# Moving a kernel's loads and stores from SyncE's DMA queue to GpSimd's and ScalarE's: attention, mixture of experts and FFN in one program

## The chip, the cores and the metric

The kernel runs on one core of a Trainium2 chip. The core has five engines with an instruction stream each: TensorE (PE, matmuls), VectorE (DVE), ScalarE (ACT), GpSimd (POOL) and SyncE (SP). An engine works through its stream in order; an instruction that must wait for something holds all that stand behind it on that engine. DMAs are issued as instructions of SP, ACT or POOL. The metric is the time of one execution on the device in microseconds; of several runs the median counts.

## The reference

Three stages, each feeding the next, all in float32:

```
attn = softmax(q k^T / 8 + decay(f), causal) v       # 4 batches, 8 heads, 576 positions, head size 64
x    = attn as 2304 tokens of 512
e    = argmax(x w_gate)                              # one of 8 experts for each token
y    = gate(x) * (relu(x w1[e]) w2[e])               # w1: 512 x 1024, w2: 1024 x 512 for each expert
h    = y w_in                                        # 512 x 2048
g    = (a0 + a1 h + a2 h^2 + a3 h^3) / (1 + |b0||h| + |b1| h^2)
out  = g w_out                                       # 2048 x 512
```

The second FFN's weights `w_in` and `w_out` come in float64.

## The kernel before, in words

**Attention.** The 32 heads are taken in 16 pairs (`g` = 0 to 15). For each pair TensorE computes row maxima (`max_pass`, tiles `mx`), then transposed scores (`scores`, tiles `st`, two buffers), ScalarE takes the exponential into `pt`, POOL masks the diagonal, and TensorE multiplies with `v` (`pv`, tile `po`). `v_gate` multiplies `vt` by the gate's weights (tile `vg`). The loads of the next pairs (`rk`, `rq`, `v`, `vt`) and the small copies of the row maxima into `QA` are issued by SP.

**Conversion of the FFN's weights.** `w_in` and `w_out` are cut into 16 pieces. For each, `w64_load` loads 1024 KB of raw 64-bit words, `w64_square` (ScalarE) and four parts of `w64_step` (VectorE) turn it into float32 in the tile `w64m`, which has one buffer, and `w64_store` stores it to `wi_d` or `wo_d` in DRAM. A table `W64` spreads the steps over the pairs; the last 11 steps are put among the expert tiles by a list of zeros and ones, one entry for each place where `do_side()` runs. Once `in_moe` is set, the store isn't issued by the step, but by `w64_store()` at the head of the next tile.

**Routing and experts.** After three batches `tile_map(0, 3)` works out the first 6 token tiles (128 tokens of one expert each); the remaining ones follow after the fourth batch. `fetch_w(0)` then loads the first expert's weights, eight pieces of 512 KB into the tiles `raw0` to `raw7`. `scatter_to` writes the tokens' numbers into a table in DRAM, `fetch_i` and `fetch_x` (POOL) read a tile's numbers and gather its tokens (`xg`), up to five tiles ahead. `tiles()` runs over the tiles `p`: `split_some` splits `raw` into `w_hi` (ScalarE, L1029) and `w_lo` (VectorE, L1030), under a condition, where the expert changes; `h_mm` and `y_mm` are the two matmuls; `store_y(p - 1)` stores the tile before (`y_d` and the token numbers `id_d`, on SP); `fetch_next(p)` issues, under a condition, the next expert's eight loads into `raw` (SP, L497). In each tile two `do_side()` stand after the first half of the matmuls, and one or two at the end. With these inputs 22 tiles run; the branch behind L1152, for more of them, is not taken.

**FFN.** From tile 10 on, `side` holds the steps of `ffn_head`: loads of the first 512 rows of `y_d` and `id_d` (`yl`, `id`), loads of pieces of `wi_d` and `wo_d` into `rw` (four buffers), `split_w` of each (ScalarE casts to `wih` or `woh`, POOL subtracts to `wil` or `wol`), and the transposes of `yl`. After the tiles the FFN runs in five chunks of rows.

**What sets the order.** Every engine runs its instructions in the order in which the program writes them. Each DMA of SP or ACT gets one of eight semaphores DMAHW0 to DMAHW7, in turn and in common; each DMA of POOL one of DMASW0 to DMASW7. A DMA waits until the one that had its semaphore last has landed.

Of the kernel before, what the change touches and what calls it, by code (L numbers as in the profile page):

```python
# [23 lines left out]
E = 8  # L24
# [47 lines left out]
def fused_kernel(tc, q2, k2, v2, f, w_gate, w1, w2, w_in, w_out, a_in, b_in, out):  # L72
    nc = tc.nc
    with ExitStack() as top, tc.manual_schedule():
# [379 lines left out]
        got_i, got_x = set(), set()  # L454
        need = {}

        def fetch_w(p, pieces=range(NP), first=None):
            if p not in need:
                need[p] = expert(p)
            e, nd = need[p]  # L460
            for i in pieces:
                ins = fetch_piece(p, i, e, nd)
                if first is not None:
                    tc.add_manual_dep(ins.ins, first, SYNC, reason="the first tokens come before")


        def fetch_next(p):
            e = nc.sync.value_load(at(t_nx, p), min_val=0, max_val=E - 1)
            nd = nc.sync.value_load(at(t_ndx, p), min_val=0, max_val=1)
            for i in range(NP):  # L470
                fetch_piece(p, i, e, nd)


        def fetch_border(i):
            e = nc.sync.value_load(t_b[0:1, 0:1], min_val=0, max_val=E - 1)
            nd = nc.sync.value_load(t_b[0:1, i:i + 1], min_val=0, max_val=1)
            for k in range(NP):
                fetch_piece(NA, k, e, nd)

        def expert(p):  # L480
            e = nc.sync.value_load(at(t_e, p), min_val=0, max_val=E - 1)
            nd = None
            if p:
                nd = nc.sync.value_load(at(t_need, p), min_val=0, max_val=1)
            return e, nd

        def fetch_piece(p, i, e, nd):
            if True:
                if i < 4:
                    src = w1[ds(e, 1), i * P:(i + 1) * P, :].rearrange("a p f -> (a p) f")  # L490
                    dst = raw[i]
                else:
                    src = w2[ds(e, 1), (i - 4) * 256:(i - 3) * 256, :].rearrange("a (c p) d -> p (a c) d", p=P)
                    dst = raw[i].rearrange("p (c d) -> p c d", c=2)
                if nd is None:
                    return nc.sync.dma_start(out=dst, in_=src)
                return nc.sync.dma_start(out=dst, in_=src, cond=nd)  # L497

        def ffn_head(ffn, pool_, y_d, id_d, wi_d, wo_d):
            F0 = ffn["pool"]
            ffn["w", 0] = [F0.tile([P, 4, 512], F32R, name=f"{n}0") for n in ("wih", "wil", "woh", "wol")]
            ffn["yT", 0] = [F0.tile([P, 4, 512], F32R, name=n) for n in ("yhi0", "ylo0")]
# [3 lines left out]
            def load_w(q, i):  # L508
# [4 lines left out]
                else:  # L513
                    src = wo_d[q * 512 + k * P:q * 512 + (k + 1) * P, :]
                nc.sync.dma_start(out=r, in_=src)
                rw_t[q, i] = r
# [7 lines left out]
            def load_y(ci, chunk, tbs=None):  # L524
# [3 lines left out]
                for tb in range(n // P) if tbs is None else [tbs]:  # L528
                    r = slice(c0 + tb * P, c0 + (tb + 1) * P)
                    t = F0.tile([P, DM], F32, tag="yl", name=f"yl{ci}_{tb}", bufs=4)  # L530
                    nc.sync.dma_start(out=t, in_=y_d[r, :])
                    ffn["y"].append(t)
                    t = F0.tile([P, 1], I32, tag="id", name=f"id{ci}_{tb}", bufs=8)
                    nc.sync.dma_start(out=t, in_=id_d[r, :])
                    ffn["id", ci].append(t)
# [29 lines left out]
        with ExitStack() as sa:  # L565
# [19 lines left out]
            ch = DW.tile([32, 2, S], F32R, tag="w64", name="ch", bufs=2)  # L585
            rq_t, rk_t, v_t, w64_t, w64_done = {}, {}, {}, {}, []

# [77 lines left out]
            def w64_load(i):  # L665
                w = DW.tile([P, 1024, 2], I32, tag="w64", name=f"w64_{i}", bufs=2)
                nc.sync.dma_start(out=w.rearrange("p a b -> p (a b)"), in_=w64_at(i)[0].bitcast(I32))
                w64_t[i] = [w]

            def w64_store():  # L670
                for i in w64_done:
                    nc.sync.dma_start(out=w64_at(i)[1], in_=w64_t.pop(i)[2])
                w64_done.clear()
# [7 lines left out]
            def w64_step(i, part):  # L681
# [15 lines left out]
                else:  # L697
# [3 lines left out]
                    w64_done.append(i)  # L701
                    if not in_moe:
                        w64_store()

# [211 lines left out]

            in_moe = []
            first_x = [lambda p=p: (got_i.add(p), fetch_i(p)) for p in range(2)]
            first_x += [lambda p=p: (got_x.add(p), fetch_x(p)) for p in range(2)]
            W64 = [[0, 0, 0, 0, 0, 1, 0], [0, 1, 0, 1, 1, 0, 0], [0, 2, 0, 0, 2, 0, 0], [0, 2, 0, 1, 1, 0, 1], [0, 1, 1, 0, 1, 0, 0], [1, 1, 1, 0, 1, 0, 0], [1, 1, 0, 1, 1, 0, 0], [0, 1, 1, 1, 1, 0, 0], [1, 1, 1, 0, 1, 0, 0], [1, 1, 1, 0, 1, 0, 0], [0, 1, 1, 0, 1, 1, 0], [1, 1, 1, 1, 0, 0, 0], [1, 1, 1, 0, 1, 0, 0], [0, 0, 1, 0, 0, 0, 0], [0, 1, 0, 1, 0, 0, 0], [1, 1, 0, 0, 0, 1, 0]]  # L920
            for g in range(NG):
# [40 lines left out]
                if n and n % H == 0:  # L962
# [5 lines left out]
                    else:  # L968
                        steps += [slots[0], lambda c=scatters, f=slots[1]: (f(), pool_side.extend(c))]
                        steps.append(lambda: (list(tile_map(0, B - 1)), fetch_w(0), pool_side.extend(first_x)))  # L970
                    side += steps
# [39 lines left out]
            in_moe.append(True)  # L1011
            side += [lambda c=c: do_w64(c) for c in (1, 0, 1, 1, 1, 1, 1, 1, 1, 1, 1, 0, 1)]

# [3 lines left out]
        with ExitStack() as sm:  # L1017
# [39 lines left out]
            def tiles(p0, p1, always=False):  # L1057
# [3 lines left out]
                for p in range(p0, p1):  # L1061
                    if p == 10:
                        assert not side
                        w64_store()
                        st_r.close()
                        ffn["pool"] = pool(st_f, "F0", side="right")
                        side.extend(ffn_head(ffn, pool, y_d, id_d, wi_d, wo_d))
                    if p > p0:
                        store_y(p - 1)
                    w64_store()  # L1070
                    xhi, xlo = xT_t.pop(p)
# [80 lines left out]
            with tc.If(nc.values_load(at(t_start, NSURE), min_val=0, max_val=NT) < NT):  # L1152
                fetch_w(NSURE)
                fetch_ahead(NSURE, NTILE)
                tiles(NSURE, NTILE, always=True)
        st_w.close()


# [180 lines left out]
```

## Time and profile before

| | us |
|---|---|
| median of 3 runs | 1136.57 |
| the three runs | 1136.57, 1142.54, 1129.04 |
| profiled execution | 1128.95 |
| its span, first to last instruction | 1127.4 |
| PE busy in the span | 971.1 |
| DVE busy | 776.9 |
| ACT busy | 600.1 |
| POOL busy | 368.5 |

The attention takes about the first 317 us, the expert tiles run to about 695 us, and the FFN to the end. The rows of the profile that follow further below name a line of the kernel, an engine, and the tiles written and read (`out<-in`). "SPq" is SP's queue of DMA instructions. Idle time in brackets is that of the engine just before the instruction, with what ended it. The granted clock of TensorE is told as a share of full speed: 1.00 is the upper of its two levels, 0.50 the lower.

### The profile page before, as it was taken

The numbers are of one execution on the slowest core, as the hardware profiler recorded it, in microseconds if no ns is written. First come the engines' busy times: TensorE is split into PE (matmuls) and PEld (weight loads), VectorE is DVE, ScalarE is ACT, GpSimd is POOL, SyncE is SP. The second block draws the span as 40 slices with busy tenths as digits, with TensorE's granted clock in tenths as the row PEclk, the third lists the DMA queues.
The fourth block names the chain that finished last, engine by engine and source line by source line (L and its number), as shares of the span: only waits on it lengthen the run. The fifth ranks groups of instructions, "written<-read, shape, count | busy, mean of one in ns | idle before, by whom it ended". The sixth has DMA issues, their size and how long they took to land. (4 is left out here: it accounts for less than half of the span.)

```text
span 1127.4 us, 15936 instructions
## 1 busy us (share of the span) xinstructions
PE 971.1 (86%) x4965; PEld 819.1 (73%) x4965; DVE 776.9 (69%) x1412; ACT 600.1 (53%) x928; POOL 368.5 (33%) x428
## 2 busy tenths in 40 slices
PE   4989998886579873987698988889999999999996
PEld 3878887876557653765576866667888888899995
DVE  6876989977056852652326444999988887798984
ACT  6644654542134441552325344777866666677773
POOL 7663756655213020100320000575412222232222
PEclk9966988978589986998989998899999999999999
DMA  5746576777456666666836823331010020010000
GB/s 189 262 141 240 188 230 216 256 176 90 167 188 74 173 226 224 61 205 212 243 71 130 221 58 132 101 97 46 23 44 4 7 66 1 10 47 1 29 1 29
DMA packets 57231, 137.47 MB, mean 122 GB/s; under 512 B 13279, under 2 KB 13703, under 8 KB 55090
## 3 DMA queue, kind: packets, MB, share of 16 engines
q1 hardware_dynamic: 52576, 125.85, 38.0%
q0 software_dynamic: 4544, 10.52, 4.5%
q8 instruction: 41, 0.67, 0.3%
q14 instruction: 52, 0.43, 0.2%
q10 hardware_dynamic: 18, 0.00, 0.0%
HBM read 171.04 MB, written 23.86 MB: 173 GB/s over the span
## 5 line engine op out<-in xcount | busy, mean ns | idle before, releaser
L1222 POOL TENSOR_TENSOR glo<-s,ghi 128x512 fp32r<-128x512 f32 (+1 forms) x68 | 82.4, 1211 | 258.0 <-ACT ghi L1220 173.3
L1030 DVE TENSOR_TENSOR wlo<-raw,whi 128x1024 fp32r<-128x1024 f32 x88 | 104.4, 1224 | 36.5 <-ACT whi L1029 34.5
L809 PE MATMUL po<-v,pt 128*128 128x80 f32 (+2 forms) x960 | 122.7, 283 | 7.1 <-DVE lgh L820 6.9
L809 PEld LDWEIGHTS po<-v,pt 128*128 128x128 f32 (+2 forms) x960 | 115.3, 194 | 16.3 <-issue 8.2
L1183 PE MATMUL fh<-yhi,wih 128*128 128x512 f32 (+1 forms) x320 | 121.6, 380 | 5.6 <-DVE s L1200 5.5
L1185 PE MATMUL fh<-yhi,wil 128*128 128x512 f32 (+1 forms) x320 | 119.9, 375 | 0.0
L1184 PE MATMUL fh<-ylo,wih 128*128 128x512 f32 (+1 forms) x320 | 119.8, 374 | 0.0
L1237 PE MATMUL o<-woh,glo 128*128 128x512 f32 x288 | 113.8, 395 | 1.5 <-POOL glo L1222 1.5
L1235 PE MATMUL o<-woh,ghi 128*128 128x512 f32 x288 | 113.2, 393 | 0.1
L1236 PE MATMUL o<-wol,ghi 128*128 128x512 f32 x288 | 112.7, 391 | 0.0
L1029 ACT CAST whi<-raw 128x1024 fp32r<-128x1024 f32 x88 | 87.8, 1046 | 41.2 <-DMA raw<-in_dram 39.8
L782 ACT ACTIVATE pt<-st 128x768 f32<-128x768 f32 (+1 forms) x64 | 53.5, 837 | 102.2 <-PE st L779 99.1
L1195 ACT ACTIVATE s<-fh 128x512 f32<-128x512 f32 (+1 forms) x80 | 44.3, 554 | 91.3 <-PE fh L1185 91.3
L1082 PE MATMUL h<-whi,xhi 128*128 128x512 f32 x176 | 77.1, 438 | 17.6 <-ACT whi L1029 14.8
L712 DVE CUSTOM_DVE_ANT_0 junk<-mx,wide 128x512 f32<-128x512 f32 (+3 forms) x128 | 62.3, 487 | 33.9 <-PE mx L729 22.0
L1197 DVE SCALAR_TENSOR_TENSOR s<-s,bab,s 128x512 f32<-128x512 f32 (+1 forms) x80 | 56.4, 705 | 36.9 <-ACT s L1196 36.2
L1082 PE MATMUL h<-whi,xlo 128*128 128x512 f32 x176 | 72.8, 414 | 4.5 <-DVE xlo L1049 4.5
L786 POOL TENSOR_SCALAR_AFFINE_SELECT pt<-pt 128x128 f32<-128x128 f32 x144 | 45.3, 342 | 94.5 <-ACT pt L782 93.5
L434 POOL DMA_INDIRECT xg<-x_d,idx x22 | 27.9, 1270 | 140.9 <-DVE ys L1135 111.2
L1095 DVE TENSOR_TENSOR hlo<-ht,hhi 128x512 fp32r<-128x512 f32 x44 | 30.3, 688 | 61.9 <-ACTq L1038 46.6
L1086 ACT ACTIVATE hs<-h 128x512 f32<-128x512 f32 x44 | 26.2, 595 | 87.6 <-PE h L1082 87.5
L1183 PEld LDWEIGHTS fh<-yhi,wih 128*128 128x128 f32 x320 | 60.9, 190 | 15.4 <-DVE s L1200 5.9
(227 smaller groups left out, 2427.6 us busy)
## 6 DMA issues: line engine op xcount, KB each, us to landing
raw<-in_dram SPq DMA_DIRECT2D x200, 512.0 KB
w<-in_dram SPq DMA_DIRECT2D x16, 1024.0 KB
rk<-in_dram SPq DMA_DIRECT2D x16, 576.0 KB
rq<-in_dram SPq DMA_DIRECT2D x16, 576.0 KB
v<-in_dram SPq DMA_DIRECT2D x16, 368.5 KB
y_d<-ys SPq DMA_DIRECT2D x22, 256.0 KB
vt<-in_dram SPq DMA_DIRECT2D x16, 320.0 KB
yl<-y_d SPq DMA_DIRECT2D x18, 256.0 KB
```

What stands on the lines that cost most here:

```text
L712: nc.vector.tensor_tensor_reduce(out=junk[:, :n], in0=in_, in1=mask, scale=1.0, scalar=-3e38, op0=ALU.add, op1=ALU.max, accum_out=out_)
L809: nc.tensor.matmul(po[:BS[i], i, :w], lhsT=pt[r, c:c + BS[i]], rhs=v[r, (h * NB + j) * VW:(h * NB + j) * VW + w], start=(j == 0), stop=(j ...
L1029: nc.scalar.copy(out=w_hi[i], in_=raw[i])
L1030: nc.vector.tensor_tensor(out=w_lo[i], in0=raw[i], in1=w_hi[i].bitcast(F32), op=ALU.subtract)
L1082: nc.tensor.matmul(t, lhsT=x[:, k * P:(k + 1) * P], rhs=w[k][:, c], start=(i == 0), stop=(i == 11))
L1183: nc.tensor.matmul(t[:, :n], lhsT=whi[:, k, c], rhs=hi[:, k, :n], start=(k == 0), stop=False)
L1184: nc.tensor.matmul(t[:, :n], lhsT=whi[:, k, c], rhs=lo[:, k, :n], start=False, stop=False)
L1185: nc.tensor.matmul(t[:, :n], lhsT=wlo[:, k, c], rhs=hi[:, k, :n], start=False, stop=(k == 3))
L1222: eng.tensor_tensor(out=lo, in0=s3, in1=hi.bitcast(F32), op=ALU.subtract)
L1235: nc.tensor.matmul(t, lhsT=hi[:, s], rhs=whi[:, c], start=(u == 0), stop=False)
L1236: nc.tensor.matmul(t, lhsT=hi[:, s], rhs=wlo[:, c], start=False, stop=False)
L1237: nc.tensor.matmul(t, lhsT=lo[:, s], rhs=whi[:, c], start=False, stop=(u == NU - 1))
```

## The change

Four things are edited. `fetch_w(0)` is issued by ScalarE in place of SP. Once `in_moe` is set, `w64_load` and `w64_store` are issued by POOL, and the store comes right behind the step that finishes its tile; the list that places the last 11 steps is another. While `ffn["head"]` is set, which it is until the tiles are done, the loads of `yl`, `id` and `rw` are issued by POOL. In the branch that is not taken the experts' loads lose their condition.

```diff
+        def fetch_w(p, eng=nc.sync):
+            e = eng.value_load(at(t_e, p), min_val=0, max_val=E - 1)
+            for i in range(NP):
+                fetch_piece(i, e, None, eng)
...
-                    return nc.sync.dma_start(out=dst, in_=src)
-                return nc.sync.dma_start(out=dst, in_=src, cond=nd)
+                    return eng.dma_start(out=dst, in_=src)
+                return eng.dma_start(out=dst, in_=src, cond=nd)
...
-                nc.sync.dma_start(out=r, in_=src)
+                (nc.gpsimd if ffn["head"] else nc.sync).dma_start(out=r, in_=src)
                 rw_t[q, i] = r
...
-                    nc.sync.dma_start(out=t, in_=y_d[r, :])
+                    eng = nc.gpsimd if ffn["head"] else nc.sync
+                    eng.dma_start(out=t, in_=y_d[r, :])
...
-                    nc.sync.dma_start(out=t, in_=id_d[r, :])
+                    eng.dma_start(out=t, in_=id_d[r, :])
...
             def w64_load(i):
-                nc.sync.dma_start(out=w.rearrange("p a b -> p (a b)"), in_=w64_at(i)[0].bitcast(I32))
+                eng = nc.gpsimd if in_moe else nc.sync
+                eng.dma_start(out=w.rearrange("p a b -> p (a b)"), in_=w64_at(i)[0].bitcast(I32))
...
             def w64_store():
                 for i in w64_done:
-                    nc.sync.dma_start(out=w64_at(i)[1], in_=w64_t.pop(i)[2])
+                    eng = nc.gpsimd if in_moe else nc.sync
+                    eng.dma_start(out=w64_at(i)[1], in_=w64_t.pop(i)[2])
...
                     w64_done.append(i)
-                    if not in_moe:
-                        w64_store()
+                    w64_store()
...
-                        steps.append(lambda: (list(tile_map(0, B - 1)), fetch_w(0), pool_side.extend(first_x)))
+                        steps.append(lambda: (list(tile_map(0, B - 1)), fetch_w(0, nc.scalar), pool_side.extend(first_x)))
...
-            side += [lambda c=c: do_w64(c) for c in (1, 0, 1, 1, 1, 1, 1, 1, 1, 1, 1, 0, 1)]
+            side += [lambda c=c: do_w64(c) for c in (1, 1, 1, 0, 0, 1, 1, 1, 1, 0, 0, 1, 1, 1, 1)]
...
             F0 = ffn["pool"]
+            ffn["head"] = True
...
         st_w.close()
+        ffn["head"] = False
...
                 for p in range(p0, p1):
                     if p == 10:
                         assert not side
-                        w64_store()
...
                     if p > p0:
                         store_y(p - 1)
-                    w64_store()
```

The first place is the end of the attention, where the first expert's weights are loaded. On SP before, between the copies of the row maxima of the last pair but one and of the last one:

```order
L761 DMA QA_157<-mm_2472 1x9x128 [waits DMAHW0_49,DVE_49]
L481 TENSOR_LOAD te_100 [waits DVE_49]
...
L496 DMA raw_85<-in_dram 128x1024 [waits DMAHW1_49]
...
L496 DMA raw_86<-in_dram 128x1024 [waits DMAHW2_49]
...
L496 DMA raw_92<-in_dram 128x2x512 [waits DMAHW0_49]
L622 DMA v_2583<-in_dram 128x737 [waits DMAHW1_49,PE_49]
L623 DMA vt_2584<-in_dram 128x640 [waits DMAHW2_49]
L761 DMA QA_147<-mm_2690 1x9x128 [waits DMAHW3_49,Activation_49]
L761 DMA QA_147<-mm_2690 1x9x128 [waits DMAHW4_49,DVE_49]
```

On SP now (raw_85 to raw_92 are the tiles raw0 to raw7):

```order
L752 DMA QA_157<-mm_2472 1x9x128 [waits DMAHW1_49,DVE_49]
L612 DMA v_2583<-in_dram 128x737 [waits DMAHW3_49,PE_49]
L613 DMA vt_2584<-in_dram 128x640 [waits DMAHW5_49]
L752 DMA QA_147<-mm_2690 1x9x128 [waits DMAHW3_49,Activation_49]
L752 DMA QA_147<-mm_2690 1x9x128 [waits DMAHW4_49,DVE_49]
```

And on ACT now, where before the exponential of `st_0_2620` followed the copy of `v_2340` at once:

```order
L624 COPY v_2340<-vg_2499 128x5x2x8 [waits DMAHW0_49,PE_49]
L457 TENSOR_LOAD te_100 [waits DVE_49]
...
L484 DMA raw_85<-in_dram 128x1024
...
L484 DMA raw_86<-in_dram 128x1024 [waits DMAHW2_49]
...
L484 DMA raw_89<-in_dram 128x2x512 [waits DMAHW7_49]
...
L484 DMA raw_90<-in_dram 128x2x512 [waits DMAHW0_49]
...
L484 DMA raw_91<-in_dram 128x2x512 [waits DMAHW1_49]
...
L484 DMA raw_92<-in_dram 128x2x512 [waits DMAHW2_49]
L773 ACTIVATE pt_164<-st_0_2620 128x768 [waits PE_49,Pool_49]
```

The eight loads left SP, where `v` and `vt` moved ahead of them, and stand on ACT ahead of the exponentials of the pair. raw_90 waits for the semaphore that raw_85 has, raw_92 for that of raw_86.

The second place is the conversion among the expert tiles. On SP before, one of the stores stood behind two sets of eight loads of `raw` and the store of a tile:

```order
L497 DMA raw_92<-in_dram 128x2x512 [waits DMAHW3_49]
...
L1054 DMA y_d<-ys_4114 128x512 [waits DMAHW4_49,DVE_49]
...
L1055 DMA id_d<-idx_3137 128x1 [waits DMAHW5_49,DMASW0_49]
L672 DMA wo_d<-w64m_4039 128x1024 [waits DMAHW6_49]
```

On POOL now, that load and store stand among the gathers of tokens:

```order
L434 DMA xg_3738<-x_d,idx_3723 128x513 [waits DMASW1_49,DVE_49]
...
L658 DMA w_14_3821<-in_dram 128x2048 [waits DMAHW7_49]
...
L664 DMA wo_d<-w64m_3895 128x1024 [waits DVE_49]
...
L425 DMA idx_3908<-table 128x1 [waits DMAHW4_49,DMASW7_49]
L434 DMA xg_3910<-x_d,idx_3736 128x513 [waits DMASW3_49,PE_49]
```

The store moved ahead of both sets of `raw` loads and off their queue. Behind it on POOL, the next read of token numbers waits for VectorE's last step.

The third place is tile 10 and the ones after it, where the FFN's first loads are made. On POOL now:

```order
L434 DMA xg_4800<-x_d,idx_4634 128x513 [waits DMASW2_49,PE_49]
...
L521 DMA yl_0_4894<-y_d 128x512 [waits DMAHW3_49,DMASW6_49,Activation_49]
L524 DMA id_0_4896<-id_d 128x1 [waits DMAHW4_49]
L504 DMA rw_0_4898<-wi_d 128x512 [waits DMASW0_49]
...
L511 TENSOR_TENSOR wil_4809<-rw_0_4898,wih_4808 128x512 [waits Activation_49]
...
L504 DMA rw_4_5156<-wo_d 128x512 [waits DMASW4_49,Pool_49]
L511 TENSOR_TENSOR wil_4809<-rw_1_4904,wih_4808 128x512 [waits Activation_49]
...
L434 DMA xg_5171<-x_d,idx_4993 128x513 [waits DMASW7_49,DMASW6_49,DVE_49]
...
L504 DMA rw_5_5252<-wo_d 128x512 [waits Pool_49]
```

Before, these loads stood on SP, each behind the eight loads of `raw` of its tile; POOL's stream held the subtractions and gathers alone. A load of `rw` now waits on POOL itself for the subtraction that frees its buffer.

## Rows read from the trace of the kernel before

**Rows 1.** Windows of 50 us: busy time and number of instructions of each engine.
```profile
core 0: us, PE busy (x) PEld busy (x) DVE busy (x) ACT busy (x) POOL busy (x), PEclk, DMA share, GB/s
250.00:300.00 50.00, 29.88 (x200) 27.98 (x199) 23.01 (x87) 10.63 (x15) 18.39 (x33) 0.74 0.74 147
400.00:450.00 50.00, 27.66 (x106) 21.25 (x106) 20.87 (x22) 14.29 (x19) 6.07 (x6) 0.73 0.64 225
800.00:850.00 50.00, 50.00 (x223) 40.83 (x222) 43.77 (x64) 35.55 (x60) 13.17 (x15) 1.00 0.12 38
```

**Rows 2.** TensorE's timeline around its longest waits; idle time and releaser in brackets.
```profile
start us, us, engine line op out<-in xcount [idle before <-releaser]
...
269.01 0.80 PE L729 MATMUL mx<-KA,QA 128*128 128x512 f32 x1 [4.15 <-DVE M L712]
...
271.42 0.47 PE L777 MATMUL st<-QB,KB 128*128 128x192 f32 x1
...
293.18 2.37 PE L632 MATMUL vg<-wg,vt 128*128 128x64 f32 x10 [15.47 <-DMA vt<-in_dram]
...
447.12 1.12 PE L1092 MATMUL ht<-ident,hs 128*128 128x128 f32 x4 [17.27 <-ACT hs L1086]
...
500.75 0.83 PE L1092 MATMUL ht<-ident,hs 128*128 128x128 f32 x4 [4.83 <-ACT hs L1086]
...
526.45 1.11 PE L1092 MATMUL ht<-ident,hs 128*128 128x128 f32 x4 [7.93 <-ACT hs L1086]
...
564.03 1.12 PE L1092 MATMUL ht<-ident,hs 128*128 128x128 f32 x4 [8.83 <-ACT hs L1086]
```

**Rows 3.** ScalarE's timeline: one exponential, and three of its waits.
```profile
264.96 0.81 ACT L782 ACTIVATE pt<-st 128x768 f32<-128x768 f32 x1 [5.53 <-PE st L779]
...
445.46 1.12 ACT L678 ACTIVATE w64m<-w 128x1024 f32<-128x1024 f32 x1 [18.23 <-DMA wo_d<-w64m]
...
525.28 0.62 ACT L521 CAST wih<-rw 128x512 fp32r<-128x512 f32 x1 [9.38 <-DMA rw<-wi_d]
...
562.20 1.29 ACT L521 CAST woh<-rw 128x512 fp32r<-128x512 f32 x2 [9.59 <-DMA rw<-wo_d]
```

**Rows 4.** SP's timeline: issues of DMAs between 265 and 551 us.
```profile
265.35 6.62 SPq L496 DMA_DIRECT2D raw<-in_dram  x8
...
275.67 0.97 SPq L622 DMA_DIRECT2D v<-in_dram  x1
...
277.04 0.35 SPq L623 DMA_DIRECT2D vt<-in_dram  x1
...
283.42 1.83 SPq L761 DMA_DIRECT2D QA<-mm  x2
...
416.89 11.91 SPq L497 DMA_DIRECT2D raw<-in_dram  x16
...
431.62 0.33 SPq L672 DMA_DIRECT2D wo_d<-w64m  x1
...
550.90 4.12 SPq L515 DMA_DIRECT2D rw<-wo_d  x3
```

**Rows 5.** SP's waits, 250 to 350 us: in total, times, longest.
```profile
SPq L761 <- DMA raw<-in_dram: 6.2, 2, 6.0
SPq L622 <- DMA raw<-in_dram: 3.6, 1, 3.6
```

**Rows 6.** Shorter windows, the columns of Rows 1: the DMA engines, TensorE's clock.
```profile
260.00:265.00 5.00, 4.68 (x39) 4.11 (x38) 4.51 (x23) 0.04 (x1) 3.50 (x5) 1.00 0.00 0
265.00:268.00 3.00, 0.00 (x0) 0.00 (x0) 2.62 (x18) 0.78 (x1) 2.54 (x6) 1.00 1.50 22
274.00:277.00 3.00, 3.00 (x28) 2.78 (x27) 2.35 (x6) 1.91 (x4) 2.56 (x7) 1.00 1.03 394
300.00:305.00 5.00, 5.00 (x25) 4.71 (x25) 2.30 (x7) 1.20 (x2) 0.53 (x2) 0.50 0.11 45
566.00:569.00 3.00, 3.00 (x9) 2.33 (x8) 0.49 (x1) 0.50 (x1) 2.12 (x3) 0.50 0.00 0
```

**Rows 7.** POOL: a scatter, the wait behind it, and the gathers' issue (min/median/max).
```profile
275.80 1.65 POOL L113 DMA_INDIRECT table<-tok,gsi  x1 [0.16 <-issue]
...
289.47 0.60 POOL L425 DMA_DIRECT2D idx<-table  x1 [12.02 <-DMA table<-tok,gsi]
...
L434 POOL DMA_INDIRECT xg<-x_d,idx x22: 972/1001/3105, 294.9 to 622.8; - x22
```

More of the change, by code (lines that the diff above doesn't have):

```diff
@@ L454, in fused_kernel @@
         got_i, got_x = set(), set()
[L455 to L464, printed above, removed]
+        def fetch_w(p, eng=nc.sync):
+            e = eng.value_load(at(t_e, p), min_val=0, max_val=E - 1)
+            for i in range(NP):
+                fetch_piece(i, e, None, eng)
         def fetch_next(p):
@@ L470, in fetch_next @@
             for i in range(NP):
-                fetch_piece(p, i, e, nd)
+                fetch_piece(i, e, nd)
         def fetch_border(i):
@@ L477, in fetch_border, with fetch_piece @@
             for k in range(NP):
[L478 to L487, printed above, removed]
+                fetch_piece(k, e, nd)
+        def fetch_piece(i, e, nd, eng=nc.sync):
             if True:
@@ L585, in fused_kernel @@
             ch = DW.tile([32, 2, S], F32R, tag="w64", name="ch", bufs=2)
-            rq_t, rk_t, v_t, w64_t, w64_done = {}, {}, {}, {}, []
+            rq_t, rk_t, v_t, w64_t, w64_done, in_moe = {}, {}, {}, {}, [], []
             def load_k(g):
@@ L914, in do_w64 @@
                             w64_load(i + 1)
-            in_moe = []
             first_x = [lambda p=p: (got_i.add(p), fetch_i(p)) for p in range(2)]
```

## The prediction

> **What bounds the kernel now.** I read the 50 us windows first [rows 1]: from 800 us on, in the FFN, TensorE is busy 50.00 of 50 us at full clock, and nothing that this change touches can make that part shorter. In 250 to 300 us it works 29.88 us, in 400 to 450 us 27.66 us. So I went to TensorE's own timeline and looked for rows with a large idle time before them [rows 2]: 15.47 us at 293.18 for the load of vt, 17.27 us at 447.12, 7.93 us at 526.45 and 8.83 us at 564.03 for ScalarE's hs. Together 49.5 us. ScalarE's timeline tells what it was held by in the last three [rows 3]: 18.23 us for the store of w64m to wo_d, 9.38 us for a load of rw from wi_d, 9.59 us for a load of rw from wo_d. All four releasers are DMAs, all four were issued by SP, and SP's timeline shows them behind eight or sixteen loads of raw, the expert's weights [rows 4]. I call the four waits A, B, C and D. A fifth, 4.83 us at 500.75, hangs on raw itself; I count it as it is.
>
> **A, the first expert's weights.** SP issues eight raw loads from 265.35, and only then v at 275.67 and vt at 277.04 [rows 4]. The two were ready much earlier: in the changed order they stand right behind QA and before any raw, and the DMA engines moved 0 GB/s from 260 to 265 us [rows 6]. So I take A's 15.5 us as gone. What is added: the eight issues stand in ScalarE's stream, between the copy of v and the first exponential of the last pair but one. A DMA waits for the one that had its semaphore before, and in the order raw_90 waits for the number that raw_85 has, raw_92 for that of raw_86. In the run before, v and vt had the numbers next after raw_85's and raw_86's, and so show when these landed: SP waited 3.6 us for a raw before v [rows 5] and issued it at 275.67, and vt at 277.04 [rows 4]. The engines moved little until then, 22 GB/s at 265 to 268 us beside the table's scatters, and 394 GB/s only from 274 us [rows 6]. ScalarE is thus held to about 277.0 + 0.4 = 277.4 us. Its exponential that began at 264.96 [rows 3] ends at 278.2 (0.81 us long). TensorE needs the buffer that this frees for the score tile that it began at 271.42 [rows 2]: 6.8 us late. Net 15.5 - 6.8 = 8.7. After the old wait TensorE ran at 0.50 of its clock, still so at 300 to 305 us [rows 6], that is 12 us of which up to 6 could come back; a half-speed stretch will follow the new wait too, so I take 0.3. **A: -9 us.** Bounds: if raw_85 and raw_86 land at once, -15.5 - 6 = -21.5; if ScalarE is held until raw_87 has landed (SP's 6.0 us wait before QA at 283.42 [rows 4, 5]), 6.4 us less, -2.3.
>
> **B, the FFN weight's conversion.** The store of w64m waited in SP's stream behind sixteen raw loads (issued from 416.89; store at 431.62 [rows 4]), and ScalarE's next square needs the one w64m buffer. Now the store is on POOL, right behind VectorE's last step, before the raw loads; and the steps are spread so that the next square comes two tiles after the store, not one. With six steps between, even a slow store is covered. -17.3 us. Against it: w_14 (1024 KB) moves from behind one expert's raw loads to beside them. At the 394 GB/s of [rows 6] that is 2.7 us of the engines, in a tile that waits for raw; half of it, 1.3 us. VectorE's and ScalarE's steps are the same in number and only change tiles. **B: -16 us**, bounds -12 (all 2.7 us, and as much again where w_15 now runs beside raw) and -19 (half-clock time after the wait comes back).
>
> **C and D, the FFN's first loads.** Eleven rw, four yl and four id loads leave SP for POOL, where they no longer follow each tile's raw. C: the first rw is wanted by the cast that waited 9.38 us. On POOL it is issued once the y store of the tile before has landed, ahead of or beside raw. I take off 2 us for sharing. D: the three rw at 550.90 [rows 4] come behind eight raw; on POOL each goes as soon as POOL has split the tile that had the buffer, a tile sooner. After D TensorE ran at 0.50 to 569 us [rows 6], 5 us, of which 2.5 come back; C's wait is as long, so 2.5 there as an estimate. **C: 7.9 + 2.5 - 2, -8 us; D: 8.8 + 2.5, -11 us.** Bounds: 0 each, if the loads are as late on POOL as on SP, and -10.4 and -11.3.
>
> Costed at nothing: 24 more issues on POOL. A plain one takes about what a gather's does, 1.0 us as the median [rows 7], 24 us in all, on an engine that waits for VectorE in most of this stage; the cover is gone if they hold up the gathers, which run five tiles ahead. SP's 48 rows fewer, and the need loads in a branch that isn't taken (22 y stores, one a tile), are nothing as well.
>
> **Sum.** -9 - 16 - 8 - 11 = -44 us against the profiled execution's 1128.95 us: 1085 us. That one was as fast as the fastest of the three runs; their median, 1136.57, is 7.6 above it. I add half of that: **1089 us**.
>
> **A rule against it.** The trace shows four waits for DMAs that stood behind others on one queue. The Trainium skill, page "DMA: Bandwidth & Descriptors", section "Issuing engines are not separate DMA queues", says that DMAs from several engines run on the same 16 engines, and that issuing from more of them saves the sequencer's issue time alone. By it the sum would be near 0; it is the second rival below. My sum differs because here the order on the queue is what costs: vt was not slow, it was issued at 277.04.
>
> **Rivals.**
> 1. The next thing late is raw (chance 0.10). With the waits gone, TensorE reaches each change of expert sooner, and ScalarE's cast waits there instead. For: the 4.83 us at 500.75 is such a wait already. Against: where C and D lie, the raw loads aren't wanted until tiles later. C and D are then given back, and 3 us of B: -22, 1111 us.
> 2. The queues don't matter (0.08): the engines serve the moved bytes as late as before, and only issue time is saved, 6.62 us for the eight raw [rows 4], which SP had to spare. 1133 us, no change. Against: the engines stood idle just before A.
> 3. Slower (0.08): POOL's stream becomes the bound. Loads there stand in order with gathers that wait for the tile's ys, with splits of rw, and with stores that wait for VectorE. A transfer that POOL issued can take long: the scatter at 275.80 let the next step go only at 289.47, after 12.02 us of waiting [rows 7], 13.7 us from its issue, and a gather's issue took up to 3.1 us where its median is 1.0 [rows 7]. If each of tiles 10 to 13 waits once for such a round trip, that is 4 x 13.7 = 55 us in place of C's and D's 16.7; with A at its worst (-2) and B at -16 the whole is +20, and with the 3.8 us of the median 1153 us. It decides where the round trip passes (16.7 + 18) / 4 = 8.7 us. Against: that scatter ran beside 4 MB of raw and wrote single words. The Trainium skill, page "SBUF — State Buffer", section "SBUF: two separate sides", states a cause for the long issues: VectorE in a two-port mode keeps GpSimd from writing descriptors, and a DMA from ScalarE's or SP's queue is free of that. The spread of the gather's issue agrees with it.
>
> **Chances and range.** My forecast has 0.74. A measurement of this kernel tells about 1% (11 us) from no change. Forecast and first rival are faster by more than that, except for a few cases at the forecast's weak end: 0.83 faster, 0.09 within 1%, 0.08 slower. All best bounds together are -62 us, 1067; all worst ones -14 us, with the median's 7.6 us 1122. Not all will fall together: 1070 to 1113, which takes in the first rival.
>
> **What would show it.** A: no wait of TensorE for vt; in its place ScalarE idle some 12 us before an exponential, released by a raw, and TensorE waiting about 7 us for it. If ScalarE is idle for less than 3 us, the hold by semaphores was wrong. B: the squares of w64m with no wait for a store. C and D: the casts of rw with waits under 2 us, and POOL's rw loads issued before or among the tile's raw. The FFN from its first chunk to the end should take as long as before, within 3 us; if it doesn't, my split into stages is wrong. The prediction is wrong if raw waits grow by more than 10 us in total, or if TensorE waits for gathers.

## The result, and the profile after

The changed kernel took 1103.26 us (median of 4 runs, 1101.91 to 1107.63), the kernel before beside it 1139.55 us (4 runs, 1129.04 to 1145.14). The ratio is 0.9699, 95% interval 0.9619 to 0.9779: 34 us faster (25 to 43). Forecast were 1089 us, and 1070 to 1113 as the range. The profiled execution of after took 1101.91 us (span 1100.3 us), 27 us less than that of before.

The same 50 us windows as [rows 1]:

```profile
core 0: us, PE busy (x) PEld busy (x) DVE busy (x) ACT busy (x) POOL busy (x), PEclk, DMA share, GB/s
250.00:300.00 50.00, 37.88 (x280) 34.72 (x279) 25.41 (x93) 15.09 (x20) 21.18 (x41) 0.83 0.79 153
400.00:450.00 50.00, 42.28 (x194) 33.38 (x193) 23.88 (x28) 19.32 (x28) 5.73 (x9) 0.90 0.68 158
800.00:850.00 50.00, 50.00 (x229) 41.35 (x228) 40.23 (x58) 34.34 (x58) 11.64 (x9) 1.00 0.03 6
```

TensorE gained 8 us of work in the first, 14.6 us in the second, nothing in the FFN. Its timeline where [rows 2] had the long waits:

```profile
start us, us, engine line op out<-in xcount [idle before <-releaser]
...
264.79 0.80 PE L720 MATMUL mx<-KA,QA 128*128 128x512 f32 x1 [3.99 <-DVE M L703]
...
274.27 0.53 PE L768 MATMUL st<-QB,KB 128*128 128x192 f32 x1 [6.88 <-ACT pt L773]
...
283.16 1.33 PE L622 MATMUL vg<-wg,vt 128*128 128x64 f32 x10
...
438.87 0.80 PE L1070 MATMUL h<-whi,xhi 128*128 128x512 f32 x1 [7.72 <-ACT whi L1019]
...
498.44 1.11 PE L1080 MATMUL ht<-ident,hs 128*128 128x128 f32 x4 [5.79 <-ACT hs L1074]
```

The waits for vt and behind w64m are gone. In their place stand 6.88 us behind ScalarE, 7.72 us behind a cast of raw, and 5.79 us of C's old wait. ScalarE says why:

```profile
261.21 12.10 ACTq L484 DMA_DIRECT2D raw<-in_dram  x8
273.41 1.51 ACT L773 ACTIVATE pt<-st 128x768 f32<-128x768 f32 x2 [18.05 <-DMA raw<-in_dram]
...
437.77 5.78 ACT L1019 CAST whi<-raw 128x1024 fp32r<-128x1024 f32 x6 [10.11 <-DMA raw<-in_dram]
...
451.16 1.19 ACT L670 ACTIVATE w64m<-w 128x1024 f32<-128x1024 f32 x1 [0.19 <-ACTq L1028]
...
497.27 0.62 ACT L510 CAST wih<-rw 128x512 fp32r<-128x512 f32 x1 [7.20 <-DMA rw<-wi_d]
...
525.54 0.62 ACT L510 CAST woh<-rw 128x512 fp32r<-128x512 f32 x1 [5.46 <-DMA rw<-wo_d]
```

To see where each microsecond came and went, I took the start of the scaling that writes `ys`, once per tile, and noted how far each kernel is ahead of before there (us; four profiled executions, alone = one part of the change by itself, below).

| point (start in before) | after | A alone | B alone | C and D alone |
|---|---|---|---|---|
| matmul of unchanged attention (269.01) | 4.2 | 4.3 | -2.9 | 2.9 |
| tile 3 (383.83) | 15.1 | 15.1 | -1.6 | 3.7 |
| tile 5 (422.13) | 15.6 | 15.5 | 0.7 | 4.1 |
| tile 6 (453.24) | 34.4 | 13.1 | 19.5 | 2.1 |
| tile 8 (479.04) | 20.8 | 12.8 | 6.2 | 2.1 |
| tile 10 (510.80) | 25.9 | 12.2 | 12.8 | 0.5 |
| tile 11 (536.11) | 25.6 | 11.6 | 9.7 | 5.2 |
| tile 12 (547.50) | 22.3 | 11.7 | 9.7 | 4.0 |
| tile 13 (571.33) | 32.4 | 11.5 | 8.2 | 13.0 |
| tile 15 (601.76) | 29.7 | 11.6 | 8.2 | 10.7 |
| tile 21 (694.90) | 29.1 | 14.7 | 8.0 | 11.0 |

The first line is what the executions differ by before anything changed; A is the step after it, 10.9 us. B's wait gives 18.8 us at tile 6, and tiles 7 and 8 take 13.6 us of it back. Tile 10 wins 4.9 us (the fifth wait, at 500.75 in [rows 2], is gone), D wins 10.1 us at tile 13, and C (tile 11) nothing in after. From tile 21 to the end 2 us are lost. So of the 27 us between the two profiled executions the change made about 23; the other 4.2 were there before it began.

What holds the cast at 437.77? SP's timeline, from the tile before:

```profile
start us, us, engine line op out<-in xcount [idle before <-releaser]
...
402.35 13.73 SPq L485 DMA_DIRECT2D raw<-in_dram  x16
417.74 0.37 SPq L1044 DMA_DIRECT2D y_d<-ys  x1
418.36 0.37 SPq L1045 DMA_DIRECT2D id_d<-idx  x1
420.64 12.12 SPq L485 DMA_DIRECT2D raw<-in_dram  x8
434.70 0.37 SPq L1044 DMA_DIRECT2D y_d<-ys  x1
435.31 0.36 SPq L1045 DMA_DIRECT2D id_d<-idx  x1
437.59 7.08 SPq L485 DMA_DIRECT2D raw<-in_dram  x8
```

and what the DMA engines did meanwhile (columns as above; the last two are their busy share, where 1.00 is all 16, and what they moved):

```profile
411.00:425.00 14.00, 14.00 (x72) 11.48 (x70) 6.92 (x8) 4.76 (x8) 2.08 (x3) 1.00 1.01 387
425.00:433.00 8.00, 6.16 (x30) 4.77 (x28) 1.38 (x2) 1.48 (x3) 0.54 (x1) 1.00 0.96 56
433.00:436.00 3.00, 0.00 (x0) 0.00 (x0) 0.00 (x0) 0.00 (x0) 1.00 (x1) 0.76 0.19 70
```

The expert's 4 MB are in by 425: 14 us at 387 GB/s are 5.4 MB, and later there are no 4 MB at all. The packet records hold all its rows by then. (The share adds up the time of all packets in the records, so it can pass 1.00.) Then the engines are busy (0.96) and move almost nothing (56 GB/s), for 8 us. I call this crawling. In the trace's records of single packets, 14 of the 15 such stretches counted further below begin within 3 us of the writing of a tile's 128 token numbers, 4 bytes each, to id_d. [rows 6] had shown one already: a share of 1.50 at 22 GB/s from 265 to 268, beside the scatters into the table, which write 4 bytes per token. Each tile's loop ends in eight raw loads that are mostly skipped by their condition; the cast waits for SP to have come past them, skipped or not. And SP is held there, because these issues share eight semaphores with the two stores ahead of them (the order of after's SP stream, one tile):

```
L1044 DMA y_d<-ys_3306 128x512 [waits DMAHW3_49,DVE_49]
L1045 DMA id_d<-idx_2763 128x1 [waits DMAHW4_49,DMASW0_49]
...
L485 DMA raw_91<-in_dram 128x2x512 [waits DMAHW3_49,DVE_49,Activation_49]
L485 DMA raw_92<-in_dram 128x2x512 [waits DMAHW4_49,DVE_49,Activation_49]
```

So the eight issues from 420.64 last 12.12 us, 7.1 us of it a wait for the y_d store; the next y_d store is out only at 434.70, the next raw issue at 437.59, the cast at 437.77. That is the theory that the second set of runs tests. Until then I had: order on a queue costs (A, B, C, D are each late by what stands ahead), against the rival that queues don't matter and against the prediction's own sizes.

### The profile page after: what moved, and what is told of

It reads as the page before. It is cut to its first block, busy times and chain, and to the rows that moved or that the text cites. A ratio compares the mean times of both kernels' runs of the same rounds, so it can differ in the third digit from the quotient of the medians.

```text
span 1100.3 us, 15948 instructions
## 1 busy us (share of the span) xinstructions
PE 961.6 (87%) x4965; PEld 804.7 (73%) x4965; DVE 781.2 (71%) x1412; ACT 600.2 (55%) x928; POOL 379.0 (34%) x452
## 5 line engine op out<-in xcount | busy, mean ns | idle before, releaser
L800 PE MATMUL po<-v,pt 128*128 128x80 f32 (+2 forms) x960 | 115.9, 274 | 5.1 <-DVE lgh L811 4.9
L800 PEld LDWEIGHTS po<-v,pt 128*128 128x128 f32 (+2 forms) x960 | 109.1, 184 | 14.1 <-issue 6.2
L1019 ACT CAST whi<-raw 128x1024 fp32r<-128x1024 f32 x88 | 87.5, 1047 | 55.5 <-DMA raw<-in_dram 51.9
L1070 PE MATMUL h<-whi,xhi 128*128 128x512 f32 x176 | 80.0, 454 | 29.1 <-ACT whi L1019 28.0
L768 PE MATMUL st<-QB,KB 128*128 128x192 f32 (+3 forms) x208 | 69.0, 348 | 7.1 <-ACT pt L773 7.1
L1172 PEld LDWEIGHTS fh<-yhi,wih 128*128 128x128 f32 x320 | 60.7, 190 | 15.1 <-DVE s L1189 5.7
L1070 PEld LDWEIGHTS h<-whi,xhi 128*128 128x128 f32 x176 | 36.0, 204 | 48.6 <-ACT whi L1019 42.1
```

Of the source, the lines that this page charges most:

```text
L768: nc.tensor.matmul(t[:, c:c + w], lhsT=KB[s][:, k0:k0 + P], rhs=QB[s][:, q0 + done:q0 + done + w], start=True, stop=False)
L800: nc.tensor.matmul(po[:BS[i], i, :w], lhsT=pt[r, c:c + BS[i]], rhs=v[r, (h * NB + j) * VW:(h * NB + j) * VW + w], start=(j == 0), stop=(j ...
L1019: nc.scalar.copy(out=w_hi[i], in_=raw[i])
L1070: nc.tensor.matmul(t, lhsT=x[:, k * P:(k + 1) * P], rhs=w[k][:, c], start=(i == 0), stop=(i == 11))
L1172: nc.tensor.matmul(t[:, :n], lhsT=whi[:, k, c], rhs=hi[:, k, :n], start=(k == 0), stop=False)
```

## The experiments

Each was timed in three rounds against the kernel before. Ratios stand to before; where I compare two experiments I divide their ratios. By their intervals such a quotient is uncertain by about 1%, some 11 us.

**The parts alone.** A alone passes `eng=nc.scalar` through `fetch_w`; B alone has the w64 loads and stores on `nc.gpsimd`, the store behind the last step, and the new list; C and D alone have the FFN's loads on `nc.gpsimd` until the flag falls.

```
A:     -fetch_w(0)                         +fetch_w(0, eng=nc.scalar)
B:     -for c in (1, 0, 1, 1, 1, ...)      +for c in (1, 1, 1, 0, 0, 1, ...)
       -nc.sync.dma_start(... w64_at(i))   +eng = nc.gpsimd if in_moe else nc.sync
C, D:  -nc.sync.dma_start(out=r, in_=src)  +(nc.gpsimd if ffn["head"] else nc.sync).dma_start(...)
```

> Only the first expert's weights go through ScalarE's queue; all the rest is as before. Theory (order): the 15.5 us that TensorE waited for vt at 293 go, ScalarE is held by its own eight issues and TensorE is 6 to 7 us late for that: 9 to 12 us faster, near 1128. Rival (queues don't matter, the 4 MB delay vt wherever they are issued): within 3 us of before. If this part alone carried the whole gain it would be 36 us.

1116.00 us, ratio 0.9907 (0.9873 to 0.9941): 10.5 us faster. The wait moved as in after, 6.33 us for ScalarE in place of the 15.47 for vt. As expected.

> Only the weight conversion of the MoE stage goes through GpSimd's queue, with its new list of steps; the rest is as before. Prediction's own term: 16 us faster, near 1123. Theory after seeing the changed kernel: the 17 us wait for the store goes, but the next tiles' waits for raw grow by 10 to 13 us, so 4 to 7 us faster, near 1133. Rival (the late raw comes from the other parts of the change, such as the earlier start of the stage): the full 16 us.

1114.60 us, ratio 0.9882 (0.9836 to 0.9928): 13.3 us faster, with an interval of 8 to 18 us that holds the prediction's 16 and begins just above the 4 to 7 of the theory. The trace decides: tile 6 is 18.8 us earlier, tiles 7 and 8 give 13.3 us back, as in after.

```profile
452.54 5.78 ACT L1029 CAST whi<-raw 128x1024 fp32r<-128x1024 f32 x6 [10.01 <-DMA raw<-in_dram]
```

The late raw thus belongs to B itself, not to the earlier start of the stage: the rival falls. That the gain is still larger than the theory's 4 to 7 comes from tile 10, which wins 6.

> Only the FFN's first loads go through GpSimd's queue. Prediction's own terms: 8 for wih and 11 for woh, 19 us faster, near 1120. Theory after seeing the changed kernel: wih is as late as before, because its loads stand behind yl and id on GpSimd and those wait for the y_d and id_d stores; woh's 10 us are won: 8 to 12 us faster, near 1129.

1120.12 us, ratio 0.9929 (0.9886 to 0.9973): 8.0 us faster, at the low edge of what I expected. By the table C gives 4.7 us here (tile 11) and D 8.9 (tile 13); part goes again at tiles 12 and 15. So in these single executions C alone is worth something, and after A and B it is worth nothing.

The three sum to 31.8 us, each uncertain by 4 to 5 us; the whole change is worth 34 us. Nothing large is seen to be lost between the parts.

**Same queue, other place.** Before, with the first weights on SP, one step later:

```
-steps.append(lambda: (list(tile_map(0, B - 1)), fetch_w(0), pool_side.extend(first_x)))
+steps.append(lambda: (list(tile_map(0, B - 1)), pool_side.extend(first_x)))
+steps.append(lambda: fetch_w(0))
```

> The first expert's weights stay on SyncE's queue and are issued one step later, behind v and vt; nothing else differs from before. Theory (order on the queue is what costs): TensorE's 15.5 us wait for vt goes and no engine is held by the issues: 13 to 18 us faster, near 1123, better than through ScalarE's queue. Rival (the eight loads must leave SyncE's queue): the QA loads that then stand behind them are late instead, and TensorE waits for those: 0 to 8 us faster.

1116.47 us, ratio 0.9895 (0.9847 to 0.9943): 11.8 us faster, the same as through ScalarE's queue (0.9907). vt's wait is gone and a shorter one stands behind it:

```profile
292.15 0.50 PE L779 MATMUL st<-QA,KA 128*128 128x192 f32 x1 [9.37 <-DMA QA<-mm]
```

What costs is which small transfer stands behind the 4 MB; which queue carries them makes no difference to the time that these intervals show. The price is another one, though. In the packet records QA's rows, issued here at 276.49 behind raw on the same queue, begin to move at 288.66, 12.2 us later, when raw, which crawls to about 285, is nearly through. With raw on ScalarE's queue QA was issued at 279.84 and moved from 284.05, 4.2 us later and beside raw; TensorE waited 1.30 us for it there, but 6.33 us for ScalarE. I had expected more than from ScalarE's queue, since I did not count QA, which now comes behind.

**Wider rows for the token numbers.** The changed kernel, `id_d` as `[NT + P, 16]`; same stores, same queue, same semaphores:

```
+nc.vector.tensor_copy(out=idw_t[p], in_=idx_t.pop(p).to_broadcast([P, 16]))
-nc.sync.dma_start(out=id_d[ds(o, P), :], in_=idx_t.pop(p))
+nc.sync.dma_start(out=id_d[ds(o, P), :], in_=idw_t.pop(p))
```

> The changed kernel with each tile's 128 token numbers stored as rows of 64 bytes instead of 4; number, order and queue of the stores are the same. Theory (after each store of 128 times 4 bytes all transfers crawl for 6 to 9 us, so the y_d and id_d stores land 12 to 14 us after their issue, and SyncE, whose later issues share their semaphores, comes late to the next expert's weights): the crawling is gone, the stores land within 4 us, ScalarE's waits for raw between 370 and 700 us fall from 51 us to under 20, and the kernel is 25 to 40 us faster than the changed one, near 1070. Rival (the crawling comes from the gathers or from the conversion's loads beside raw): within 3 us of the changed kernel.

1049.00 us, ratio 0.9304 (0.9240 to 0.9369); against the changed kernel 0.9304 / 0.9699 = 0.959, 45 us, more than expected. The waits of SP among the expert tiles (370 to 700 us; in total, times, longest), after (first) and with 64-byte rows (second):

```profile
SPq L485 <- DMA y_d<-ys: 30.2, 7, 7.1
SPq L485 <- DMA raw<-in_dram: 20.8, 20, 2.4
SPq L485 <- DMA id_d<-idx: 14.3, 10, 4.0
```

```profile
SPq L1044 <- DVE idw L1126: 42.6, 8, 7.2
...
SPq L485 <- DMA raw<-in_dram: 10.5, 9, 2.6
```

SP hardly waits for y_d any more (1.3 us in all) and not for id_d; it waits for VectorE to give it something to store. ScalarE's waits (300 to 700 us) for raw and rw in after and here:

```profile
ACT whi L1019 <- DMA raw<-in_dram: 51.9, 23, 10.1
ACT wih L510 <- DMA rw<-wi_d: 8.8, 2, 7.2
ACT woh L510 <- DMA rw<-wo_d: 7.5, 3, 5.5
```

```profile
ACT whi L1019 <- DMA raw<-in_dram: 11.9, 16, 3.1
```

The waits for rw are gone too. In the packet records I joined those that took over 1.2 us and followed each other within 1 us, and kept groups of four or more: between 300 and 700 us after has 15 such stretches of 4 to 10 us, about 107 us together; here there is one, at 341 to 347.

**The stores off SP.** The changed kernel, the two stores on GpSimd, still 4 bytes a row:

```
-o = nc.sync.value_load(...)                +o = nc.gpsimd.value_load(...)
-nc.sync.dma_start(out=y_d[...], ...)       +nc.gpsimd.dma_start(out=y_d[...], ...)
-nc.sync.dma_start(out=id_d[...], ...)      +nc.gpsimd.dma_start(out=id_d[...], ...)
```

> The changed kernel with the y_d and id_d stores of each tile issued by GpSimd; their sizes stay. Theory (SyncE is late because its issues wait for those stores): the transfers crawl as before, but SyncE no longer waits for them, so the waits for raw shrink: 10 to 25 us faster than the changed kernel, near 1085. Rival (raw is late because its transfer is slow): no gain; and GpSimd, with two issues more per tile, may bring the gathers late: up to 10 us slower.

1072.83 us, ratio 0.9487 (0.9422 to 0.9553); 0.978 of the changed kernel, 24 us. The crawling stayed, as it should (21 stretches by the same count, 137 us). ScalarE's waits for raw fell to 30.4 us, with a longest of 11.8:

```profile
443.79 5.78 ACT L1019 CAST whi<-raw 128x1024 fp32r<-128x1024 f32 x6 [11.85 <-DMA raw<-in_dram]
```

That one is the tile that gave B back, and it did not improve. Here the transfer itself met the crawling: 161 GB/s from 419 to 426, and 38 GB/s from 435 to 443. So crawling makes raw late in two ways, by holding SP and by slowing the bytes; about half the gain can be had without touching its cause.

**rw ahead of yl and id.**

```
-steps = [lambda n=n: (load_y(0, first, n), load_w(*ws[n])) for n in range(4)]
+steps = [lambda n=n: load_w(*ws[n]) for n in range(4)]
 steps += [lambda n=n: step_w(n) for n in range(8)]
+steps += [lambda n=n: load_y(0, first, n) for n in range(4)] + [lambda: None] * 2
```

> The changed kernel with the FFN's first weight loads (rw) issued ahead of the loads of yl and id, which follow after all eight conversions. Theory (part C won nothing because rw_0 stood on GpSimd behind yl and id, and those behind the landing of y_d and id_d): rw lands 10 us earlier and the 6 to 8 us that TensorE waits behind wih near 498 go: 5 to 9 us faster than the changed kernel, near 1095. Rival (rw is late because its transfer meets the crawling after an id_d store): under 3 us.

1097.28 us, ratio 0.9702 (0.9640 to 0.9765), which the intervals can't tell from the changed kernel's 0.9699. In the trace wih's and woh's waits for rw are gone, and by tile 14 the kernel has won 16.8 us on after since tile 0; at tile 15 it loses 7.6 of them again. The place of the wait is shown, its price in the whole is not.

**The token number in the y_d row.** The changed kernel without id_d stores: `ys` and `y_d` have 16 columns more, which hold the number, and `id` is loaded from there.

```
-ys = M.tile([P, DM], ...)                  +ys = M.tile([P, DM + 16], ...)
+nc.vector.tensor_copy(out=ys[:, DM:].bitcast(I32), in_=idx_t.pop(p).to_broadcast([P, 16]))
-nc.sync.dma_start(out=id_d[ds(o, P), :], in_=idx_t.pop(p))
```

> The changed kernel with the token numbers stored as the last 64 bytes of the y_d rows (2112 bytes each), so there is no id_d store; they are loaded from there. Theory: as with 64-byte rows, and one issue and one shared semaphore fewer per tile: 25 to 42 us faster than the changed kernel, near 1067. Rival: within 3 us of it.

1048.31 us, ratio 0.9281 (0.9221 to 0.9342). This is the lowest ratio of all kernels here, 0.957 of the changed kernel; the one with 64-byte rows and the two with 2052-byte rows and three buffers below can't be told from it.

> The changed kernel with the token number as the last 4 bytes of y_d rows of 2052 bytes, which begin and end off the 64-byte grid. Theory 1 (it is the row of 4 bytes by itself that makes the transfers crawl): as with rows of 2112 bytes, near 1050. Theory 2 (it is every row that does not fill whole 64-byte pieces): the crawling stays after each y_d store, and the time is near the changed kernel's, 1085 to 1103.

The same with one column more instead of 16 (rows of 2052 bytes): 1049.52 us, ratio 0.9308 (0.9267 to 0.9349). Theory 1: it is the row of 4 bytes by itself. A longer row that ends off the grid does no harm here that the time shows; ScalarE's waits for raw stay at 11.6 us. By the count above it has five stretches, 18 us together, where the kernel with 16 columns has three, 9 us together.

**The kernel before with 64-byte rows**, with nothing of the change:

> The kernel before, with nothing of the change, and the token numbers stored as rows of 64 bytes. Theory (B, C and D cured waits that the crawling after the 4-byte stores had made): wih and woh come in time on SyncE's queue too, the w64m store waits for raw issues that are no longer held, and only vt's 15 us wait stays: 10 to 20 us above the changed kernel with 64-byte rows, near 1064. Rival (the order on SyncE's queue costs its 34 us by itself): 30 to 40 us above it, near 1084.

1076.60 us, ratio 0.9527 (0.9477 to 0.9576): between the two. The change on top of it is worth 0.9304 / 0.9527 = 0.977, about 25 us, with an uncertainty of some 9 us that reaches into both expectations. The waits decide, and by them my theory was half right. vt's wait stays whole, as expected, and B's stays for the most part:

```profile
294.50 2.37 PE L632 MATMUL vg<-wg,vt 128*128 128x64 f32 x10 [15.61 <-DMA vt<-in_dram]
...
437.54 1.11 PE L1092 MATMUL ht<-ident,hs 128*128 128x128 f32 x4 [11.05 <-ACT hs L1086]
```

The store of w64m behind sixteen raw issues costs 11.05 us with the crawling gone, 17.27 with it [rows 2]; ScalarE's waits for wih and woh are 4.4 and 4.6 us instead of 9.4 and 9.6. Taken by the difference, about half to two thirds of each is order, the rest crawling.

**The routing table in 64-byte rows.** The scatters ahead of the expert tiles write 4 bytes per token as well; on top of the number in y_d, the table has 16 columns, and each scatter's source is a small tile, first one buffer, then three.

```
-table = dram.tile([NSLOT, 1], I32)          +table = dram.tile([NSLOT, 16], I32)
+tw = R2.tile([P, 16], I32, tag="tw", bufs=1)     (second run: bufs=3, filled by iota)
+nc.gpsimd.tensor_copy(out=tw, in_=tok[...].to_broadcast([P, 16]))
```

> The changed kernel with the token numbers in the y_d rows and, besides, the routing table kept as rows of 64 bytes, so that the scatters ahead of the MoE stage write 64 bytes per token instead of 4. Theory (the same crawling, 259 to 267 and 269 to 279 us, holds the first expert's weights and so ScalarE's issues): both stretches go, ScalarE is held under 6 us, TensorE's 6.5 us wait at 274 goes, and the scatters of the earlier batches free v and QA too: 6 to 20 us faster than without it, near 1037. Rival (ScalarE is held by the 4 MB at 390 GB/s): no more than 3 us.

1057.04 us, ratio 0.9352 (0.9302 to 0.9401), 8 us slower than without it, at the edge of what the two intervals can tell. The two crawls between 259 and 287 us that the other kernels with wide id rows still had were gone, but GpSimd's copy had to wait for the scatter that still read the one buffer, and TensorE for GpSimd's masks:

```profile
269.28 0.19 POOL L250 COPY tw<-tok 128x16 int32<-128x16 int32 x1 [12.01 <-DMA table<-tw,gsi]
```

```profile
275.35 4.56 PE L805 MATMUL po<-v,pt 128*128 128x80 f32 x20 [7.57 <-POOL pt L782]
```

> The changed kernel with the token numbers in the y_d rows and the table in rows of 64 bytes, whose sources are now three buffers that GpSimd fills with iota, where the run before had one and GpSimd waited up to 12 us for the scatter before. Theory: GpSimd no longer comes late to the attention's masks, ScalarE is held less by the first weights: 3 to 10 us faster than with the token numbers in y_d alone, near 1043. Rival (the scatters land late because they stand beside the 4 MB of weights, so three buffers wait as well): same as it or up to 8 us slower.

1047.94 us, ratio 0.9288 (0.9250 to 0.9325): by its median the loss is gone, and nothing is won over the number in y_d (0.9281). ScalarE's eight issues took 5.59 us instead of 11.72 with the number in y_d alone, and TensorE's 6.49 us wait behind ScalarE went as expected; a new one of 3.86 us behind VectorE stands at 276.11. The place gains and the attention ahead of it loses. Up to the exponential at 253 us of before, both executions with the wide table lost 7.4 to 7.6 us against before, where that with the number in y_d had won 3.6. From there to 303 us three buffers win 18.1 us, the number in y_d alone 10.1. The loss comes with the wide table, and its cause was not pursued.

## Why the prediction was right, and where not

**A, -9.** Right: 10.9 us in the trace, 10.5 us by itself. The eight issues held ScalarE (12.10 us of issue, 18.05 idle), and TensorE waited 6.88 us where 6.8 was forecast. The semaphores of the issues gave that number; that the raw loads landed so late was in turn the crawling after the scatters, as the run with three buffers, where the hold is gone, points to. The two waits alone make 8.6 us. The clock fits the rest, where 0.3 us had been put for it: in before TensorE ran at 0.50 from 293 to 305, in after at 0.63 from 275 to 283 and at 1.00 from 283 to 295. One reading was wrong: "vt was not slow, it was issued at 277.04". TensorE began to wait for it at 277.71, behind the issue, and in the packet records vt moves only from 289.85, when raw on the same queue is nearly through. In after it moves 1.0 us behind its issue.

**B, -16.** The step that failed. The wait itself went as said (18.8 us at tile 6 for 17.3). What failed is the entry against it: 1.3 us for w_14 beside raw in a tile that waits for raw, with rival 1 at 0.10 because "where C and D lie, the raw loads aren't wanted until tiles later", which says nothing of B's tiles. In fact raw took 13.6 us back, and not through bandwidth shared with w_14: its bytes were in by 425. SP came late to the issues that the cast waits for, held by the landing of the tile before's y_d store for 7.1 us. Rival 2 took SP's 6.62 us for eight raw issues in [rows 4] as issue time, and B never asks what the 11.91 us for sixteen wait for. SP's waits show it in before too, 30.6 us behind y_d and 11.2 us behind id_d between 255 and 700 us. The whole of B is 13.3 us by itself; in after it is 5.7 us from tile 3 to tile 8, and 4.9 at tile 10.

**C, -8.** Failed in after, for a reason that the prediction names and puts at nothing (its 2 us are for sharing): "issued once the y store of the tile before has landed". On GpSimd rw_0 stood behind yl and id:

```profile
482.71 0.55 POOL L521 DMA_DIRECT2D yl<-y_d  x1 [11.09 <-DMA y_d<-ys]
489.34 0.53 POOL L524 DMA_DIRECT2D id<-id_d  x1 [6.07 <-DMA id_d<-idx]
489.86 0.54 POOL L504 DMA_DIRECT2D rw<-wi_d  x1
```

The id_d store of 512 bytes, issued at 480.27, let GpSimd go at 489.34. The lower bound of 0 was the answer.

**D, -11.** Right: 10.1 us at tile 13.

**The fifth wait**, counted as unchanged, went with B's new places: 4.9 us.

**Costed at nothing.** The 24 issues on GpSimd (0.53 to 0.55 us each in the rows above, and no wait of TensorE for a gather) and the FFN (2 us lost, within the 3 us named) were right.

**The sum.** -44 us against 34 measured (27 between the two profiled executions). The text's own sign of failure, raw waits that grow by over 10 us, came true: ScalarE's waits for raw are 39.8 us in before and 51.9 in after, between 300 and 700 us. The sign for C and D failed as well: the casts of rw waited up to 7.20 us, not under 2. The outcome lies between the forecast and rival 1 (1111), and rival 1 was what happened to B, with its place wrong. That the time lies inside the range is no merit of B and C: the range had been drawn to take in rival 1. Rival 2 is out by the runs. Rival 3's price, a round trip over 8.7 us, was there (9 us for id_d), but it came once on GpSimd and not in four tiles.

**The rule.** The Trainium skill, page "DMA: Bandwidth & Descriptors", section "Issuing engines are not separate DMA queues", was half borne out: once vt stands ahead of the 4 MB, SyncE's own queue does as well in time as ScalarE's (0.9895 and 0.9907). What it says of the gain, issue time alone, does not cover these runs: with the crawling among the expert tiles gone, the change was still worth 25 us, and the packets of vt and QA show the loss behind the issue, on the shared queue.

**Not settled.** Why a store of 128 times 4 bytes makes all transfers slow for 4 to 10 us. In the packet records the 4-byte packets themselves take 9 ns as the median; it is many of the packets of 2 to 8 KB beside and behind them, most of 4 KB, that take 2 to 3 us, where one of 4096 bytes otherwise takes 0.16. The Trainium skill, on the same page, section "Why small descriptors are slow (HBM only)", counts an overhead per packet and 32 bytes of descriptor; that would make the small ones slow, and no run here shows that as the cause. Nor is it only rows of 4 bytes: with the table widened, the store of x_d (576 rows of 2052 bytes, issued at 145.43 and 145.88 in the run with one buffer) was followed by this stretch:

```profile
149.00:158.00 9.00, 7.52 (x58) 6.87 (x58) 8.74 (x16) 4.42 (x6) 7.94 (x8) 0.93 1.14 70
```

With three buffers it was 77 GB/s in the same window. But the store does not do it by itself: with the number in y_d and the narrow table, the same store, issued at 139.90 and 140.35, was followed by 226 GB/s from 143 to 149 and by no packet over 1.2 us. The 128 rows of 2052 bytes in y_d cost no time that can be measured. What decides, the size of a row, its place or how many there are, was not tried further.

## What to carry to other kernels

Before moving a DMA from a queue, ask what the instructions behind it there wait for, semaphores included: a long row of issues is often a row of waits, and the next thing late is found in them. A store that is tiny in bytes can be the largest cost of a stage; look for stretches in which the DMA engines are busy and move little, and for what was written just before. Give per-row numbers a place in a row that is stored anyway.

## What the hardware showed that I had not expected

- A store of 128 rows of 4 bytes to DRAM was in most tiles followed by 4 to 10 us in which transfers moved 38 to 161 GB/s in place of 390; with 128 rows of 64 bytes, or of 2052 with the 4 at their end, the time shows no such loss. In this kernel that was 45 us of 1103, give or take some 12.
- Loads whose condition skips them are not free: in order on SP's queue they waited up to 7.1 us for the semaphores of unrelated stores, and held a cast whose data had landed 12 us earlier.
- A small load issued behind 4 MB on the same queue moved only when nearly all of the 4 MB had: vt 12.8 us behind its issue, QA 12.2 us. On another queue than the 4 MB, QA moved 4.2 us behind its issue, beside them.
- Scatters with one source buffer held GpSimd for up to 12.01 us, which waited for the scatter to land before it could fill the buffer again.
